# Moving the addition of D into the filter from VectorE to GpSimd, with a new order of all instructions

## Chip, cores and metric

The kernel runs on one core of one Trainium2 chip. The metric is the device time of one execution in microseconds (us). The core has TensorE (PE, matrix products), VectorE (DVE), ScalarE (ACT), GpSimd (POOL) and SyncE (SP), which here only issues transfers (DMA). The engines run side by side, each through its own list of instructions in order, and wait for each other by semaphores.

## What is computed

Two branches share one normalized input. Branch A is a short convolution of `k` with four taps, times `v`, and then a causal convolution along the whole sequence of 2048 with a filter `ssm_k` per channel, computed by FFT in the reference. A skip term `kv * ssm_D` is added to it. Branch B is a gated feed-forward layer with 1792 hidden columns.

```python
def _A_ref(q, k, v, shift_k, ssm_k, ssm_D):
    ...
    kv = k_shift * v
    ...
    y = irfft(rfft(pad(kv)) * rfft(pad(ssm_k)))[:S]      # shortened
    y = y + kv * ssm_D[None, None, :]
    return q * y

def _B_ref(x, w_gate, w_up, w_down):
    g = x @ w_gate; u = x @ w_up                          # shortened
    return (_gelu(g) * u) @ w_down

xn = _layernorm(A_q)
s = _A_ref(xn, A_k, A_v, A_shift_k, A_ssm_k, A_ssm_D)
g = _silu(_B_ref(xn, B_w_gate, B_w_up, B_w_down))
return A_q + s * g
```

Adding `kv * ssm_D` to a convolution is the same as adding `ssm_D` to the filter's first coefficient. The kernel does that: before the filter is transformed, D (512 values) is added to its row 0.

## The kernel before

The sequence is laid out as 128 partitions by 16 tiles. The feed-forward branch runs in four quarters `q` of four tiles each. A unit `(q, m)` is a pair of products for 128 hidden columns, `xnT` with `Wg` and with `Wu`, four matrix products each (both are recorded at the helper line L641); ScalarE applies gelu (L1194), VectorE multiplies (L1203 from PSUM, L1200 from a copy). `down(q)` multiplies with `Wd`, and L1235 and L1237 finish the gate.

The convolution is a Fourier transform in stages. The filter `Hn` is transposed on TensorE (L916) into `HTr`, evicted from PSUM by ScalarE (L632) or VectorE (L635). Stage 1 multiplies two-partition-halves of it with the matrix `F1` (L959 for the filter, in eight units; L950 for `kv`), with the array split in half ("half-array mode"); `ZH` and `ZK` are stored to memory in between (L614 issues, from ScalarE's queue for ZH and SP's for ZK) and loaded again as `BH` and `BK`. Stage 2 (L1028) uses 32 by 32 tiles of the array. VectorE multiplies the spectra (L1131, L1154), L1028 also goes back (`MI`), `ZI` is stored and loaded as `BI`, and L1278 ends the inverse.

`h_fold` (L930) is the addition of D. It works on one partition: 512 values of row 0 of `HTr`, every second element, and `Drow`. It needs the front evictions of all four blocks of the filter, and only the filter's unit 0 of stage 1 reads what it writes.

The short convolution has VectorE multiply and add over 2048 columns (L1005, L1009, L1011, L1013); its taps `SKB` are spread out by four GpSimd copies (L986) from `SKR`. The layer norm of quarter 0 goes tile by tile, the others by quarter: statistics (L849, L850, VectorE), `(var + eps)^-0.5` (L862, GpSimd), `NB_` (L866), the tile (L870 ScalarE or L871 VectorE), and a transpose into `xnT`: for quarter 0 on TensorE (L892), else by a DMA that SP issues (L884).

Nothing is ordered by loops when it runs. The functions add tasks to a list (`S.add`), each with the engines that it may use, a planned time, and the buffers that it reads and writes. `SEQ`, a string, lists all 809 tasks in the order in which they are emitted; the suffix `b` takes a task's second engine. So SEQ sets the order on every engine, SP's and ScalarE's queues of transfers included, and the engine of each eviction. `Sched.run` goes through it with planned times and from them picks the PSUM banks and buffer slots. `LAND` holds the times at which the planner takes each early load to have landed; the order of the loads stands in `ORDER`. Waits are derived from what is read and written (`Trk`).

Of the kernel before, what the change touches and what calls it, by code (L numbers as in the profile page):

```python
# [11 lines left out]
ALU = mybir.AluOpType  # L12
# [12 lines left out]
N_WARM = 13  # L25
ORDER = "x00 x01 w0 D0 h0 w1 h1 h2 h3 s0 k0 w2 x1 k1 k2 w3 d0 d1 v0 v1 k3 v2 v3 x2 x3"
SEQ = (
# [22 lines left out]
)  # L50
NF_BANKS = 4
ISSUE = 470.0
LAND = {"x0_0": 3800, "h0": 8050, "x0_1": 4900, "D": 6750, "wg0": 5850, "wu0": 6700, "h1": 12450, "wg1": 9600, "wu1": 11100, "h2": 13800, "h3": 15150, "sk": 17800, "kh1": 19200, "kh113": 19400, "kz": 10800, "k0": 20600, "wg2": 22500, "wu2": 24050, "x1": 25400, "k1": 26750, "k2": 28100, "wg3": 29650, "wu3": 31200, "wd0": 33450, "wd1": 35700, "v0": 37050, "v1": 38400, "k3": 39750, "v2": 41100, "v3": 42450}
W_XT, W_SW, W_BK, W_BH, W_ZI, W_BI, W_ZK, W_MI, W_G1 = 765000, 735000, 667000, 688000, 274000, 714000, 690000, 329000, 150000
NC_PAIRS = 4
SMALL = 1.15 * 262144
# [357 lines left out]
def build_kernel(nc, A_q, A_k, A_v, A_shift_k, A_ssm_k, A_ssm_D, B_w_gate, B_w_up, B_w_down, out):  # L414
    with ExitStack() as es0:
# [11 lines left out]
        def new(name, shape, dt):  # L427
            h = at(name, shape, dt, place["at"])
            place["at"] += size(shape, dt)
            return h  # L430
# [24 lines left out]
        Drow = new("Drow", [1, DM], BF16)  # L455
# [64 lines left out]
        def dsem(name):  # L520
            return DSem(nc.alloc_semaphore(name), name)
# [91 lines left out]
        def dma(eng, out_ap, in_ap, sem, r, w):  # L613
            trk.dma(eng, lambda e: e.dma_start(out=out_ap, in_=in_ap), sem, r=r, w=w)  # L614
# [3 lines left out]
        def load(name, out_ap, in_ap, w_res, w_buf, nbytes, ring="SP", r=(), rb=()):  # L618
            sem = dsem("d_" + name)
            last_load[0] = S.add([("loads", ISSUE)], lambda e: dma(ring, out_ap, in_ap, sem, r, w_res), r=rb, w=w_buf, nbytes=nbytes, land=float(LAND[name]))  # L620

        def op(engs, fn, r=(), w=(), rr=(), ww=(), lat=0.0, after=()):

            def emit(e):
                R = rr() if callable(rr) else rr
                W = ww() if callable(ww) else ww
                trk.op(e, lambda h: fn(e, h), r=R, w=W)
            return S.add(engs, emit, r=r, w=w, lat=lat, after=after)
# [297 lines left out]
        for k in range(KD):  # L926
            h_transpose(k)
        HT0 = HTr[0:1, 0, :].rearrange("p (d c) -> p c d", c=2)[:, 0, :]
        bFold = B("fold")
        h_fold = op([("DVE", 420.0)], lambda e, h: h.tensor_tensor(HT0, HT0, Drow[:], ALU.add),  # L930
                    r=[bHD, *[bHTr[k][0] for k in range(KD)]], w=[bFold], rr=[R_D, *R_HTr[0]], ww=R_HTr[0])
        t_ln = ln(0)
        S.add([("ACT", 1900.0)], m_turn, r=[bMF], w=[bMF2])
# [388 lines left out]
def bass_recurrent_scan__ssm_conv_h3__glu_gated_geglu__prompt_kernel(  # L1322
    nc: bass.Bass,
    A_q: bass.AP,
    A_k: bass.AP,
    A_v: bass.AP,
    A_shift_k: bass.AP,
    A_ssm_k: bass.AP,
    A_ssm_D: bass.AP,
    B_x: bass.AP,  # L1330
    B_w_gate: bass.AP,
    B_w_up: bass.AP,
    B_w_down: bass.AP,
    out: bass.AP,
):
    build_kernel(nc, A_q, A_k, A_v, A_shift_k, A_ssm_k, A_ssm_D, B_w_gate, B_w_up, B_w_down, out)
# [28 lines left out]
```

## Time and profile before

| what | value |
|---|---|
| median of 3 runs | 189.29 us (189.12 to 190.32) |
| profiled execution, its own time | 189.28 us |
| its span, first to last instruction | 187.5 us |
| granted TensorE clock | 0.999 |
| TensorE / VectorE / ScalarE / GpSimd busy | 97% / 88% / 75% / 7% |
| moved by DMA | 48.37 MB |

In the profile, PE rows are matrix products and PEld rows weight loads. A row of the timeline gives start and duration in us, engine, line of the kernel, operation, and what is written and read; `x4` means four such instructions merged. Matrix products overlap, so the durations of neighbouring rows do too, and starts are the better measure. `<-` in brackets names what ended an idle time. A row that ends with "DMA to landing" gives the times from the issue of a transfer until its data was there.

### The profile page before, as it was taken

What the parts mean: (1) busy time and instruction counts of PE and PEld (TensorE: products, weight loads), DVE (VectorE), ACT (ScalarE), POOL (GpSimd) and SP (SyncE); (2) the same over time, 40 slices, a digit from 0 to 9 for tenths busy, and PEclk for the clock granted to TensorE, in tenths of its full rate; (3) what the DMA queues carried; (4) which work ended last, traced back from release to release, by engine and by line L of the source; (5) the groups of instructions that cost most, each with busy time, mean ns of one, the idle gap of its engine ahead of it and who ended that gap; (6) DMA issues with size and microseconds to landing.
All of it is one profiled execution on the core that took longest, in us unless ns stands there. A gap on an engine that the chain in (4) does not pass through costs nothing.

```text
span 187.5 us, 3669 instructions
## 1 busy us (share of the span) xinstructions
PE 182.2 (97%) x1451; PEld 80.5 (43%) x1459; DVE 164.8 (88%) x249; ACT 140.0 (75%) x193; POOL 12.9 (7%) x26
## 2 busy tenths in 40 slices
PE   8899999999999999999999999999999999999993
PEld 3585443444334344334434433434333334445552
DVE  6897999999999999969459999998899994468995
ACT  3766697898698979888878779888887863144961
POOL 4502304100000000020200000000000000000000
PEclk9999999999999999999999999999999999999999
DMA  5999999999938695777999991869327056699226
GB/s 156 352 404 299 373 374 377 394 404 245 326 87 330 225 337 212 241 260 241 290 268 261 352 343 65 298 229 334 108 111 277 0 168 217 228 325 385 83 101 235
DMA packets 38502, 48.37 MB, mean 258 GB/s; under 512 B 9427, under 2 KB 28119, under 8 KB 38486
## 3 DMA queue, kind: packets, MB, share of 16 engines
q1 hardware_dynamic: 31958, 39.76, 64.1%
q10 hardware_dynamic: 6528, 8.39, 12.6%
q8 instruction: 11, 0.18, 0.5%
q14 instruction: 5, 0.04, 0.1%
HBM read 27.39 MB, written 14.68 MB: 224 GB/s over the span
## 4 chain that ended last, share of the span: by engine, by line
PE 91%; DVE 3%; DMA 2%; ACT 1%; issue 1%; POOL 0%
PE psall L641 71%; PE psall L1224 6%; PE psall L1028 6%; PE psall L950 2%; PE psall L959 2%; PE psall L916 2%; PE psall L1278 2%; DMA X<-in_A_q_dram 2%; ACT BO L632 1%; DVE stats L849 1%; DVE KAC L1005 1%; PE psall L892 0%; DVE XN L871 0%; DVE XN L965 0%; DVE HT L1203 0%
## 5 line engine op out<-in xcount | busy, mean ns | idle before, releaser
L641 PE MATMUL psall<-xnT,Wu 128*128 128x512 bf16 (+1 forms) x248 | 56.5, 359 | 0.0
L641 PE MATMUL psall<-xnT,Wg 128*128 128x512 bf16 (+1 forms) x248 | 55.8, 359 | 0.0
L1194 ACT ACTIVATE GE<-psall 128x512 bf16<-128x512 f32 x54 | 31.9, 606 | 13.6 <-PE psall L641 11.1
L641 PE MATMUL psall<-Wd,HT 128*128 128x512 bf16 (+1 forms) x174 | 38.3, 367 | 0.8 <-issue 0.6
L1203 DVE TENSOR_TENSOR HT<-psall,GE 128x512 bf16<-128x512 f32 x43 | 29.3, 682 | 7.8 <-PE psall L641 7.5
L641 PEld LDWEIGHTS psall<-xnT,Wu 128*128 128x128 bf16 x248 | 22.5, 98 | 26.1 <-issue 2.3
L641 PEld LDWEIGHTS psall<-xnT,Wg 128*128 128x128 bf16 x248 | 21.8, 98 | 26.0 <-issue 3.2
L632 ACT ACTIVATE BO<-psall 128x1024 bf16<-128x1024 f32 x20 | 19.9, 1022 | 9.4 <-PE psall L1278 4.8
L641 PEld LDWEIGHTS psall<-Wd,HT 128*128 128x128 bf16 x182 | 16.3, 98 | 21.2 <-issue 3.9
L1131 DVE TENSOR_TENSOR HSW<-KB,HSW 128x2048 bf16<-128x2048 bf16 x16 | 19.3, 1218 | 1.9 <-ACT KB L632 1.9
L632 ACT ACTIVATE HSW<-psall 128x1024 bf16<-128x1024 f32 x15 | 15.2, 1024 | 2.4 <-PE psall L1028 2.1
L632 ACT ACTIVATE KB<-psall 128x1024 bf16<-128x1024 f32 x15 | 14.6, 1026 | 0.8 <-PE psall L1028 0.8
L1011 DVE TENSOR_TENSOR KAC<-KAC,KTM 128x2048 bf16<-128x2048 bf16 x12 | 14.6, 1217 | 0.0
L1009 DVE TENSOR_TENSOR KTM<-KK,SKB 128x2048 bf16<-128x2048 bf16 x12 | 14.6, 1215 | 0.0
L632 ACT ACTIVATE AST<-psall 128x1024 bf16<-128x1024 f32 x12 | 12.1, 1032 | 0.9 <-PE psall L950 0.8
L1224 PE MATMUL psall<-Wd,HT 128*64 128x512 bf16 (+1 forms) x112 | 12.5, 366 | 0.0
L862 POOL TENSOR_TENSOR mv<-mv,NHALF 128x1 f32<-128x1 f32 (+1 forms) x7 | 7.3, 1049 | 68.6 <-DVE mv L850 48.0
L1235 ACT ACTIVATE G<-psall 128x512 bf16<-128x512 f32 x12 | 7.1, 597 | 6.3 <-PE psall L641 6.3
L849 DVE BATCH_NORM_STATS2 stats<-X 128x6 f32<-128x512 bf16 x16 | 10.5, 675 | 0.5 <-DMA X<-in_A_q_dram 0.5
L632 ACT ACTIVATE XN<-psall 128x1024 bf16<-128x1024 f32 x9 | 9.2, 1028 | 1.1 <-PE psall L959 1.0
L1237 DVE SCALAR_TENSOR_TENSOR G<-G,psall 128x512 bf16<-128x512 bf16 x12 | 7.9, 682 | 2.3 <-ACT G L1235 2.3
L1131 DVE TENSOR_TENSOR KB<-KB,HSW 128x2048 bf16<-128x2048 bf16 x8 | 9.7, 1219 | 0.1
(91 smaller groups left out, 178.3 us busy)
## 6 DMA issues: line engine op xcount, KB each, us to landing
BH<-ZH SPq DMA_DIRECT2D x8, 512.0 KB, 5.0
HSW<-HSW SPq DMA_DIRECT2D x16, 256.0 KB, 3.7
BK<-ZK SPq DMA_DIRECT2D x8, 512.0 KB, 5.9
ZI<-BO ACTq DMA_DIRECT2D x16, 256.0 KB, 2.8
BI<-ZI SPq DMA_DIRECT2D x8, 512.0 KB, 8.5
ZK<-AST SPq DMA_DIRECT2D x6, 512.0 KB, 2.9
ZH<-XN ACTq DMA_DIRECT2D x5, 512.0 KB, 4.3
Hn<-in_A_ssm_k_dram SPq DMA_DIRECT2D x4, 512.0 KB, 8.0
```

Source lines behind the costliest of these rows:

```text
L632: return h.activation(o, i, ACTF.Copy, scale=scale)
L641: return h.matmul(o, lhsT=l, rhs=r, start=st, stop=sp)
L849: t_stats[t] = op([("DVE", 670.0)], lambda e, h, t=t: h.bn_stats(stats[:, t, :], X[:, t, :]), r=[bX[q][t % 4]], w=[bst[t]], rr=[R_X[t]], w ...
L862: t_pw = op([("POOL", 2500.0 if q else 600.0)], lambda e, hd, ts=ts, n=n: hd.tensor_tensor(mv[:, ts, 3:4], mv[:, ts, 2:3], NHALF[:, 0:n, : ...
L1009: op([("DVE", dur)], lambda e, h, j=j, m=m: h.tensor_tensor(KTM[:, m.slot, :, :], kk(j), sk(j), ALU.mult), r=need + [bSKB[j], a], w=[m], r ...
L1011: op([("DVE", dur)], lambda e, h, m=m: h.tensor_tensor(KAC[:, a.slot, :, :], KAC[:, a.slot, :, :], KTM[:, m.slot, :, :], ALU.add), r=[m], ...
L1028: trk.op("PE", lambda h: h.matmul(ps(s, i)[b, :], lhsT=wt(col)[a, :], rhs=data(col)[a, :], start=n < 16, stop=n >= len(todo) - 16, tile_po ...
L1131: return hd.tensor_tensor(pair(KB, *(2 * DM * z for z in slots())) if to else x, k, x, ALU.mult)
L1194: op([("ACT", act(512))], lambda e, h: h.activation(GE[:, g.slot, :], bank(pg), ACTF.Gelu_apprx_tanh), r=[pg], w=[g], rr=lambda: R_bank(pg ...
L1203: op([("DVE", dve(512, 1))], lambda e, h: h.tensor_tensor(HT[:, q % 2, m, :], bank(pu), GE[:, g.slot, :], ALU.mult), r=[pu, g], w=[bHT[q][m]],
L1224: trk.op("PE", lambda h, m=m, i=i, c=c: h.matmul(pc()[c, :], lhsT=HT[:, q % 2, m, 128 * jt + 64 * i:128 * jt + 64 * i + 64], rhs=Wd[:, m, ...
L1237: op([("DVE", dve(512, 1))], lambda e, h, g=g, pc=pc: h.scalar_tensor_tensor(out=g, in0=g, scalar=1.0, in1=pc(), op0=ALU.add, op1=ALU.mult ...
```

## The change

Three things change in the program's text. `h_fold` may only run on GpSimd instead of only on VectorE (with a planned 1200 ns). `LAND` gets other planned landings for the first loads; `ORDER` and so the order of the loads stays. `SEQ` is another list of the same 809 tasks.

```diff
 SEQ = (
-    "0 16 17 18 19 20 21 22 ... 44 45 2 4 1 7 3 5 10 8 11 65 9 66 73b 74 12 67 68 76 77 75 6 69 "
...
+    "0 16 17 18 19 20 21 22 ... 44 45 2 7 10 4 8 1 9 3 11 6 65 66 67 68 5 73b 74 76 77 12 75 69 "
...
-LAND = {..., "h0": 8050, ..., "sk": 17800, "kh1": 19200, "kh113": 19400, ..., "k0": 20600, "wg2": 22500, "wu2": 24050, "x1": 25400, "k1": 26750, "k2": 28100, ...}
+LAND = {..., "h0": 8150, ..., "sk": 17450, "kh1": 18600, "kh113": 18850, ..., "k0": 20100, "wg2": 21600, "wu2": 23100, "x1": 24400, "k1": 25650, "k2": 27000, ...}
...
-        h_fold = op([("DVE", 420.0)], lambda e, h: h.tensor_tensor(HT0, HT0, Drow[:], ALU.add),
+        h_fold = op([("POOL", 1200.0)], lambda e, h: h.tensor_tensor(HT0, HT0, Drow[:], ALU.add),
```

Beside the fold, 25 tasks change engine between VectorE and ScalarE, nearly all of them evictions from PSUM and normalized tiles. On GpSimd the fold comes after the four SKB copies and before the first L862 of four columns; the two identity matrices, and the four copies among themselves, change places. On TensorE the first three tasks stay, and from the fourth on the order differs by up to 24 places. On SP, the loads of BH and the transfers of the spectra (HW, BK, ZK) change places in part: BH for spectrum block 5 now comes ahead of the first two BK instead of behind the transpose of quarter 3.

More of the change, by code (lines that the diff above doesn't have):

```diff
@@ L52 @@
 ISSUE = 470.0
-LAND = {"x0_0": 3800, "h0": 8050, "x0_1": 4900, "D": 6750, "wg0": 5850, "wu0": 6700, "h1": 12450, "wg1": 9600, "wu1": 11100, "h2": 13800, "h3": 15150, "sk": 17800, "kh1": 19200, "kh113": 19400, "kz": 10800, "k0": 20600, "wg2": 22500, "wu2": 24050, "x1": 25400, "k1": 26750, "k2": 28100, "wg3": 29650, "wu3": 31200, "wd0": 33450, "wd1": 35700, "v0": 37050, "v1": 38400, "k3": 39750, "v2": 41100, "v3": 42450}
+LAND = {"x0_0": 3850, "h0": 8150, "x0_1": 4950, "D": 6750, "wg0": 5800, "wu0": 6650, "h1": 12450, "wg1": 9650, "wu1": 11150, "h2": 13750, "h3": 15050, "sk": 17450, "kh1": 18600, "kh113": 18850, "kz": 10800, "k0": 20100, "wg2": 21600, "wu2": 23100, "x1": 24400, "k1": 25650, "k2": 27000, "wg3": 29650, "wu3": 31200, "wd0": 33450, "wd1": 35700, "v0": 37050, "v1": 38400, "k3": 39750, "v2": 41100, "v3": 42450}
 W_XT, W_SW, W_BK, W_BH, W_ZI, W_BI, W_ZK, W_MI, W_G1 = 765000, 735000, 667000, 688000, 274000, 714000, 690000, 329000, 150000
```

44 rows, old and new, of the table SEQ are left out of this document.

## The prediction

> **What bounds the kernel now.** I read the page's first two parts and its chain, then the busy time by windows, then what TensorE itself waited for.
>
> ```profile
> span 187.5 us, 3669 instructions
> PE 182.2 (97%) x1451; PEld 80.5 (43%) x1459; DVE 164.8 (88%) x249; ACT 140.0 (75%) x193; POOL 12.9 (7%) x26
> PEclk9999999999999999999999999999999999999999
> ...
> PE 91%; DVE 3%; DMA 2%; ACT 1%; issue 1%; POOL 0%
> ```
>
> TensorE (PE) is busy for 97% of the span at full granted clock, and the chain that ended last is TensorE for 91%. VectorE (DVE) is second with 88%, so it can make TensorE wait for a moment, but it isn't the bound. The windows show how little idle time there is to win (columns: stretch and its length, then each engine's busy time):
>
> ```profile
> 7.20:23.20 16.00, 15.96 (x146) 11.01 (x146) 13.86 (x27) 10.02 (x17) 4.01 (x6) 1.00 1.05 358
> ...
> 168.70:184.60 15.90, 15.90 (x159) 8.85 (x158) 14.93 (x27) 10.52 (x12) 0.00 (x0) 1.00 0.57 211
> sum 177.40, PE 176.20 PEld 78.56 DVE 158.54 ACT 135.74 POOL 9.10; mean PE 35.24 PEld 15.71 DVE 31.71 ACT 27.15 POOL 1.82
> ```
>
> From 7.2 us to its last product TensorE is idle for 177.40 - 176.20 = 1.2 us. Ahead of 7.2 us lies the first wait of the waits of TensorE:
>
> ```profile
> PE psall L892 <- DVE XN L871: 0.5, 1, 0.5
> PE psall L959 <- DVE HT L1203: 0.3, 1, 0.3
> ```
>
> The first, 0.5 us, is the second normalized tile; VectorE does the same work in the same order up to that tile in both versions, and GpSimd only makes its second identity earlier, in the 2.3 us that it waits ahead of the first L862 (its row is below), so it stays. The second is where VectorE is late. Any new order is therefore played for 1.2 us of idle time, plus what TensorE loses when it changes its array mode, which the windows count as busy:
>
> ```profile
> 28.20 1.03 PE L641 MATMUL psall<-xnT,Wg 128*128 128x512 bf16 x4
> 29.07 1.03 PE L641 MATMUL psall<-xnT,Wu 128*128 128x512 bf16 x4
> 30.03 0.61 PE L959 MATMUL psall<-HTr,F 64*128 64x512 bf16 x4
> 30.57 1.04 PE L641 MATMUL psall<-xnT,Wg 128*128 128x512 bf16 x4
> ```
>
> Start to start, four full products take 29.07 - 28.20 = 0.87 us. Ahead of the half-array products of L959 it is 0.96, and these four (two passes of one product's 0.87/4 = 0.217) take 0.54 instead of 0.43. One visit to the half-array mode costs 0.09 + 0.11 = 0.20 us beside its products.
>
> **The change, part by part.** The terms are set against the profiled execution's own 189.28 us (span 187.5 and 1.8 around it), which is within 0.01 of the median of the runs, 189.29.
>
> *The fold leaves VectorE.* It is one instruction, and its queue ahead of the TensorE wait is this:
>
> ```profile
> 17.53 1.06 DVE L930 TENSOR_TENSOR HTr<-HTr,Drow 1x512 bf16<-1x512 bf16 x1
> 18.50 0.67 DVE L1203 TENSOR_TENSOR HT<-psall,GE 128x512 bf16<-128x512 f32 x1
> ...
> 23.16 0.67 DVE L1203 TENSOR_TENSOR HT<-psall,GE 128x512 bf16<-128x512 f32 x1
> 23.18 0.39 PE L959 MATMUL psall<-HTr,F 64*128 64x512 bf16 x2
> 23.88 0.39 PE L959 MATMUL psall<-HTr,F 64*128 64x512 bf16 x2 [0.31 <-DVE HT L1203]
> ```
>
> VectorE has no pause from the fold to the gating L1203 at 23.16. Without 1.06 us of work ahead of it the second L959 pair would start 23.88 - 23.18 - 0.22 = 0.48 us earlier. The new order also moves kinds of work between ScalarE and VectorE here, so the gain lies between 0 and 0.48; I take 0.2.
>
> *The fold arrives on GpSimd.* There it stands behind the four SKB copies and ahead of the first four-column power of L862. GpSimd's rows:
>
> ```profile
> 17.35 2.90 POOL L986 COPY SKB<-SKR 128x512 bf16<-128x512 bf16 x4 [8.09 <-DMA SKR<-in_A_shift_k_dram]
> 30.62 3.06 POOL L862 TENSOR_TENSOR mv<-mv,NHALF 128x4 f32<-128x4 f32 x1 [10.38 <-DVE mv L860]
> L862 POOL TENSOR_TENSOR mv<-mv,NHALF 128x1 f32<-128x1 f32 x4 | 2.3, 564 | 3.5 <-ACT mv L859 2.3 <-DVE mv L860 1.2
> ```
>
> No row has this shape on GpSimd. The bounds are its nearest two-input instructions, 0.56 us below and 3.06 us above; since the copies of 512 columns take about 0.7 each, I take 1.5. The fold can start at 17.35 + 2.90 = 20.25 and ends between 20.8 and 23.3. Its first reader, the front half of filter unit 0, is the 62nd task of TensorE in the new order (the 66th before). In the old order the 62nd task is the first of this row:
>
> ```profile
> 38.99 0.81 PE L641 MATMUL psall<-Wd,HT 128*128 128x512 bf16 x3
> ```
>
> Cover: from 23.3 to 38.99, over 15 us of other products; without it the fold's whole 0.56 to 3.06 us would fall on TensorE. The next GpSimd instruction isn't due before 30.62, over 7 us later. So its cost there is 0. No DMA moves with it.
>
> How it meets VectorE is another matter. The fold took 1.06 us on VectorE beside the copies, where its neighbour of the same width over all partitions, two-input and SBUF to SBUF, took 0.42; and the power at 30.62 took 3.06 us beside two long VectorE products:
>
> ```profile
> L1245 DVE TENSOR_TENSOR G<-G,XN 128x512 bf16<-128x512 bf16 x3 | 1.3, 418 | 0.0
> 30.46 1.20 DVE L1005 TENSOR_TENSOR KAC<-KK,SKB 128x2048 bf16<-128x2048 bf16 x1
> 31.60 1.21 DVE L1011 TENSOR_TENSOR KAC<-KAC,KTM 128x2048 bf16<-128x2048 bf16 x1
> ```
>
> The power ends at 33.68, 0.9 us after the second of them. The Trainium skill, SBUF - State Buffer, section "Who interferes with whom", says that VectorE with two SBUF inputs and a GpSimd instruction that reads SBUF exclude each other for a whole instruction, whichever issued first. By that rule, with which both rows agree, the fold could hold up VectorE by as much as it frees.
>
> Whatever the reason, a fold of 1.5 us that holds up VectorE for its length would turn the 0.2 us above into a loss; that is a rival below.
>
> *The plan's landings.* LAND only feeds the planner; no load is issued in another order. Its numbers put nothing on the chip by themselves: 0.
>
> *The order.* I compared both SEQ lists engine by engine, and laid the old one beside the trace. The first and the last of the 15 old visits to the half-array mode:
>
> ```profile
> 15.73 0.39 PE L959 MATMUL psall<-HTr,F 64*128 64x512 bf16 x2
> 78.22 0.61 PE L950 MATMUL psall<-V,F 64*128 64x512 bf16 x4
> ```
>
> TensorE keeps its 252 tasks; the new list visits that mode 13 times, the other modes as often as before. Two visits at 0.20 are -0.4 us. Nothing hides this: it is TensorE's own time. That is the surest term.
>
> At the end the cover is the same: after the last inverse product 61 products stand ahead of the first L1278 both times, so the ZI stores and BI loads have their 13 us.
>
> ```profile
> 159.97 5.25 SPq L614 DMA_DIRECT2D BI<-ZI x8
> 168.72 0.62 PE L1278 MATMUL psall<-BI,G 128*64 128x512 bf16 x4
> ```
>
> The place where the new order can lose is the SP queue near 95 us. There the third transpose of XN waits for four normalized tiles, and the spectrum load BK for TensorE's L1028 stands right behind it:
>
> ```profile
> 93.01 0.82 ACT L870 ACTIVATE XN<-X,NB__69,mv 128x512 bf16<-128x512 bf16 x1
> 95.12 1.02 ACT L632 ACTIVATE KB<-psall 128x1024 bf16<-128x1024 f32 x1
> 94.53 3.79 SPq L884 DMA_TRANSPOSE xnT<-XN  x1
> 98.37 1.13 SPq L614 DMA_DIRECT2D BK<-ZK  x2
> 94.52 0.43 PE L1028 MATMUL psall<-BK,TF 32*32 32x512 bf16 x16
> 104.99 0.43 PE L1028 MATMUL psall<-BK,TF 32*32 32x512 bf16 x16
> DMA to landing us min/median/max: 5.9/5.9/5.9
> DMA to landing us min/median/max: 4.0/4.0/4.0
> ```
>
> The last two rows are the landing of the first BK at 98.37 and of an earlier BK at 86.62. Before, BK lands at 98.37 + 5.9 = 104.2 and TensorE takes it at 104.99. In the new order one normalized tile (XN9) stands on ScalarE behind the eviction of the L1028 of 94.52. That L1028 itself moves up by the five products that now follow it, 5 x 0.217 = 1.1 us, to 93.4. Its eviction by ScalarE (1.02 in the row of KB, begun some 0.4 after the product, once ScalarE's own instruction before it is done) ends near 94.9, XN9 (0.82) near 95.7; the transpose is issued 1.2 us later than before, BK at 99.6, and it lands between 99.6 + 4.0 = 103.6 and 99.6 + 5.9 = 105.5. TensorE comes there at 104.99 less what it has won by then, 104.4 with -0.6. The new wait is 0 to 1.1 us; the middle of the landings, 104.5, gives 0.1. One 512 KB load that stood between the two transposes (BH, issued at 92.21 before) now goes ahead of both, which speaks for the lower half; I take 0.2. Behind that wait stand all of TensorE's products; what is late next is nothing, since the BK loads after it have more room.
>
> *Sum.* 189.28 - 0.4 (two visits) - 0.2 (fold's queue) + 0.2 (BK) = **188.9 us**.
>
> **The rivals.**
>
> *Everything kept.* The wait at 23.88 vanishes whole and BK is in time: 189.28 - 0.4 - 0.48 = **188.4**. For it: both are shown in rows. Against it: the old order, made in the same way, has one such wait, and this one would have none.
>
> *BK decides (the other side).* If it lands at 105.5, TensorE goes on at 105.5 whatever it has won before, for it only waits longer: 189.28 + 105.5 - 104.99 = **189.8**. The deciding point is an issue of the transpose later than about 94.9: past that each microsecond is one of the end. For it: XN9 behind the eviction; against it: the smaller queue.
>
> *The move doesn't do what it says.* The fold on GpSimd blocks VectorE for its 1.5 us in the same stretch, and the L1203 of 23.16 comes up to 1.5 - 1.06 = 0.4 later: 189.28 - 0.4 + 0.4 = **189.3**. For it: the stretched rows. Against it: the copies leave gaps, and nothing says that the same L1203 gates TensorE in the new order.
>
> *PSUM hand-overs.* Many results change engines, and a bank that waits for one more eviction in an engine's queue costs 1.0 us (the row of KB). The old order shows one such wait in 252 tasks. Three of them would be 189.28 - 0.4 + 3 x 1.0 = **191.9**; the traces can't exclude it.
>
> **How the numbers follow.** Forecast as summed 0.47; everything kept 0.16; BK decides 0.15; fold blocks VectorE 0.10; hand-overs 0.10; better than 187.4, 0.02. A change of 1% is 1.9 us, and about what a measurement of this kernel can tell from no change; the runs shown lie from 189.12 to 190.32. Faster by that needs 187.4, that is all 1.2 us of idle time, the visits and part of the front wait together: 0.02. The first four cases are all within 1%: 0.88. Hand-overs: 0.10 for slower. The range goes from 188.1 (everything kept, and 0.3 of the other idle time) to 190.3 (BK decides and half an eviction more), with no more than 2 in 10 outside.
>
> **What would show it.** TensorE's groups L959 and L950 form 13 stretches; no TensorE wait on L1203 near 23 us, or a shorter one; one L930 on GpSimd ending before 24 us with no waiter; the third transpose issued near 95.7, BK's L1028 within 0.5 us of 104.5; TensorE idle 0.9 to 1.6 us after 7.2. The forecast is wrong if TensorE's idle time there exceeds 3 us, if a filter unit waits for L930, or if the number of stretches hasn't fallen.

## The result and the profile after

The changed kernel takes **191.59 us** (median of 6 runs, 190.86 to 194.89), the kernel before 189.38 beside it (6 runs, 189.06 to 190.32). The ratio is 1.0123, 95% interval 1.0096 to 1.015: slower by 1.2%, against a forecast of 188.9 and a range that ended at 190.3. (The ratios in this document are of undisturbed runs alone, so they can lie below the ratio of the medians.) The profiled execution took 191.84 us, span 190.1, 2.6 more than before.

The waits of TensorE, first view of after (columns: who waits, for what; us in total, times, longest):

```profile
PE psall L892 <- DVE XN L871: 1.2, 2, 0.7
PE psall L1028 <- ACT BO L632: 1.1, 1, 1.1
PE psall L641 <- PEq L1350: 0.8, 1, 0.8
PE psall L959 <- ACT X L632: 0.6, 1, 0.6
...
PE psall L959 <- ACT GE L1194: 0.2, 1, 0.2
PE psall L916 <- DMA Hn<-in_A_ssm_k_dram: 0.2, 1, 0.2
```

The wait for VectorE's L1203 that before had on L959 is gone, as predicted. Three waits for evictions stand in its place, into X, into BO and into GE. (The 0.7 us more on XN costs nothing: it lies ahead of the first normalized tile, where TensorE has run only products of a constant, and the first product of data starts at 6.38 us, at 6.32 before.) The busy time by windows says where they lie. First before (columns: stretch and its length, busy time of PE, PEld, DVE, ACT and POOL, granted clock, DMA share, GB/s):

```profile
7.20:40.00 32.80, 32.40 (x223) 18.22 (x225) 30.34 (x53) 24.67 (x38) 7.08 (x7) 1.00 1.06 372
40.00:56.00 16.00, 15.95 (x81) 6.20 (x80) 16.00 (x21) 13.56 (x21) 0.00 (x0) 1.00 0.86 248
56.00:124.00 68.00, 67.63 (x546) 27.11 (x547) 60.63 (x87) 57.56 (x79) 2.03 (x2) 1.00 0.81 264
124.00:136.00 12.00, 12.00 (x128) 4.75 (x127) 10.92 (x13) 9.84 (x14) 0.00 (x0) 1.00 0.67 223
```

The same stretches of after, with the sum up to the same distance from the end:

```profile
7.20:40.00 32.80, 32.11 (x222) 17.94 (x222) 29.13 (x50) 26.74 (x43) 7.06 (x8) 1.00 1.06 374
40.00:56.00 16.00, 15.26 (x74) 6.36 (x75) 15.45 (x20) 11.27 (x16) 0.00 (x0) 1.00 1.04 260
...
124.00:136.00 12.00, 10.90 (x122) 4.26 (x121) 10.59 (x12) 9.26 (x13) 0.00 (x0) 1.00 0.66 225
...
sum 180.00, PE 176.68 PEld 78.82 DVE 159.06 ACT 136.37 POOL 9.09; mean PE 35.34 PEld 15.76 DVE 31.81 ACT 27.27 POOL 1.82
```

TensorE's idle time from 7.2 us to its last product is 180.00 - 176.68 = 3.3 us; before it was 1.2. Of the 2.1 us more, 0.3 come by 40 us, 0.7 from 40 to 56, and 1.1 from 124 to 136. (TensorE's busy time, 176.68 instead of 176.20, makes up the rest of the 2.6.) The chain of work that ended last, from 40 to 51 us of after (start, us, what), shows what is behind the middle one:

```profile
40.83 0.92 ACT X L632
...
41.78 8.03 DMA ZH<-X
...
49.83 1.03 ACT X L632
...
50.91 0.39 PE psall L959
```

Halves of X and XN serve as the four buffers from which the filter's units are stored (H buffers). The store of unit 6 (ZH6) out of a half of X is issued at 41.78 and takes 8.03 us. Only then may ScalarE evict the next unit (ps1H4) into that half, and TensorE's second pair of unit 7 waits for the bank that this eviction frees. In the chain of before there is nothing but TensorE in this stretch: there the same store was issued at 43.35 and had landed after 4.2 us, at 47.6, when its buffer was asked for at 47.96.

A second profile of the same kernel has the same wait, longer, and the BO wait shorter:

```profile
PE psall L959 <- ACT X L632: 2.3, 1, 2.3
...
PE psall L1028 <- ACT BO L632: 0.5, 1, 0.5
```

### The profile page after: what moved, and what is told of

Same layout as the page of the kernel before. It is cut to its first block, busy times and chain, and to the rows that moved or that the text cites. A ratio compares the mean times of both kernels' runs of the same rounds, so it can differ in the third digit from the quotient of the medians.

```text
span 190.1 us, 3675 instructions
## 1 busy us (share of the span) xinstructions
PE 182.0 (96%) x1449; PEld 80.7 (42%) x1459; DVE 165.2 (87%) x247; ACT 140.6 (74%) x194; POOL 13.0 (7%) x27
## 4 chain that ended last, share of the span: by engine, by line
PE 75%; DMA 10%; ACT 6%; DVE 4%; SPq 3%; issue 1%; ACTq 0%
PE psall L641 57%; PE psall L1224 6%; DMA Hn<-in_A_ssm_k_dram 6%; PE psall L1028 6%; DMA ZH<-X 4%; SPq L614 3%; PE psall L950 2%; PE psall L1278 2%; ACT BO L632 2%; ACT XN L870 1%; DVE KTM L1009 1%; PE psall L959 1%; ACT X L632 1%; ACT GE L1194 1%; DVE stats L849 1%
## 5 line engine op out<-in xcount | busy, mean ns | idle before, releaser
L641 PE MATMUL psall<-xnT,Wu 128*128 128x512 bf16 (+1 forms) x248 | 55.8, 359 | 0.0
L641 PE MATMUL psall<-xnT,Wg 128*128 128x512 bf16 (+1 forms) x248 | 55.7, 359 | 0.0
L641 PE MATMUL psall<-Wd,HT 128*128 128x512 bf16 (+1 forms) x172 | 38.5, 366 | 0.8 <-issue 0.5
L1203 DVE TENSOR_TENSOR HT<-psall,GE 128x512 bf16<-128x512 f32 x43 | 29.3, 684 | 9.9 <-PE psall L641 9.4
L1194 ACT ACTIVATE GE<-psall 128x512 bf16<-128x512 f32 x54 | 31.3, 603 | 8.7 <-PE psall L641 5.2
L641 PEld LDWEIGHTS psall<-xnT,Wu 128*128 128x128 bf16 x248 | 22.1, 98 | 26.8 <-issue 3.5
L641 PEld LDWEIGHTS psall<-xnT,Wg 128*128 128x128 bf16 x248 | 22.0, 98 | 26.1 <-issue 2.3
L641 PEld LDWEIGHTS psall<-Wd,HT 128*128 128x128 bf16 x182 | 16.4, 98 | 20.8 <-issue 2.7
L632 ACT ACTIVATE BO<-psall 128x1024 bf16<-128x1024 f32 x21 | 20.9, 1024 | 5.1 <-PE psall L641 2.1
L632 ACT ACTIVATE KB<-psall 128x1024 bf16<-128x1024 f32 x14 | 13.9, 1028 | 3.7 <-PE psall L1028 3.6
L1235 ACT ACTIVATE G<-psall 128x512 bf16<-128x512 f32 x12 | 7.0, 596 | 12.1 <-PE psall L641 12.1
L632 ACT ACTIVATE HSW<-psall 128x1024 bf16<-128x1024 f32 x14 | 13.8, 1026 | 1.5 <-PE psall L1028 1.4
L862 POOL TENSOR_TENSOR mv<-mv,NHALF 128x1 f32<-128x1 f32 (+1 forms) x7 | 6.2, 885 | 66.2 <-DVE mv L860 63.1
L1154 DVE TENSOR_TENSOR HSW<-HSW 128x2048 bf16<-128x2048 bf16 x8 | 9.6, 1216 | 0.0
```

Source lines behind the costliest of these rows:

```text
L632: return h.activation(o, i, ACTF.Copy, scale=scale)
L641: return h.matmul(o, lhsT=l, rhs=r, start=st, stop=sp)
L1154: return hd.tensor_tensor(x, x, y, ALU.add)
L1194: op([("ACT", act(512))], lambda e, h: h.activation(GE[:, g.slot, :], bank(pg), ACTF.Gelu_apprx_tanh), r=[pg], w=[g], rr=lambda: R_bank(pg ...
L1203: op([("DVE", dve(512, 1))], lambda e, h: h.tensor_tensor(HT[:, q % 2, m, :], bank(pu), GE[:, g.slot, :], ALU.mult), r=[pu, g], w=[bHT[q][m]],
```

## The experiments

The theory I began with: new waits behind stores, in the order and not in the fold's engine. The first rival: the fold on GpSimd. The second: ScalarE's queue itself.

**After, taken again.** Nothing is edited.

> The changed kernel once more. Theory (stores): its loss is made of single waits of TensorE, 1.2 us near 132 us and 0.8 us near 50 us, both behind a ScalarE eviction that waits for the buffer of a slow store, 0.6 us near 31 us, and up to 1.0 us ahead of 18 us from loads that land late; the waits at 132 and 50 come again in this profile, at about their sizes, and the time is again 191 to 192. Rival (chance of one execution): the waits stand elsewhere or are gone, and the time of the profile isn't explained by them. Whether the filter blocks land at 9.4/13.7/15.0/16.8 us again, or at 8.1/12.4/13.7/15.0 as before the change, tells whether the early 1.0 us belongs to the change.

192.22 us (190.73 to 195.24, 6 runs), ratio 1.0109 (1.0081 to 1.0138). The loss is not one run's. Its two rows stand above: the waits come again at the same places, but not at the sizes expected, 2.3 us near 50 us and 0.5 near 132. The late landings at the front that the first profile had (0.2 us on L916) did not come back.

**The fold alone, both ways.** In after the fold goes back to VectorE; in before it goes to GpSimd:

```
-        h_fold = op([("POOL", 1200.0)], lambda e, h: h.tensor_tensor(HT0, HT0, Drow[:], ALU.add),
+        h_fold = op([("DVE", 420.0)], lambda e, h: h.tensor_tensor(HT0, HT0, Drow[:], ALU.add),
```

> The changed kernel with its new order, and the fold back on VectorE. Theory (the order's waits): the fold's engine is not the cause, 191.0 to 192.0, and the waits near 50 and 132 us stay. Rival (the fold on GpSimd holds VectorE up): most of the loss is gone, 189.4 to 190.0, and the wait near 31 us is gone.

> The kernel before with its old order, and the fold alone on GpSimd behind the four copies. Theory: no loss; VectorE has 1 us less to do ahead of 23 us, so the wait there (0.48 us) shrinks: 188.8 to 189.4. Rival (the fold on GpSimd costs by itself): 190.5 or more.

After's order with the fold on VectorE: 192.15 us (191.53 to 194.08, 6 runs), ratio 1.0165 (1.0125 to 1.0204). Before's order with the fold on GpSimd: 190.1 us (189.56 to 190.78, 12 runs), ratio 1.0035 (1.0021 to 1.0049). So the slowdown stays when the fold's move is undone, and the move alone costs 0.4 to 0.9 us on the old order, between what the theory and the rival had. The wait for L1203 is still there in that profile, 0.37 us at 24.2. Why the move gains nothing is in two rows of the timeline of before with the fold on GpSimd:

```profile
20.12 1.15 POOL L930 TENSOR_TENSOR HTr<-HTr,Drow 1x512 bf16<-1x512 bf16 x1
...
20.47 1.95 DVE L965 TENSOR_TENSOR XN<-XN 128x1024 bf16<-128x1024 bf16 x2
```

And in the line of the product L1005 in after (duration in ns, least, median and most):

```profile
L1005 DVE TENSOR_TENSOR KAC<-KK,SKB x4: 1211/1214/2179, 21.4 to 61.5; 128x2048 bf16<-128x2048 bf16 x4
```

The pair of L965 took 1.27 us in the kernel before and takes 1.95 beside the fold. In after the product L1005 that begins at 21.4, under the fold on GpSimd, takes 2.18 us instead of 1.21. VectorE gets 1.06 us of work less and is held for 0.7 to 0.97. (Why the move costs something beyond that, these rows don't show.) The Trainium skill, SBUF - State Buffer, section "Who interferes with whom", has the rule for it, an exclusive lock between VectorE with two SBUF inputs and GpSimd; both traces agree with it.

**More buffers.** Two more output buffers of the inverse (BO), then one more for the filter's spectra, then both:

```
-        BO = at("BO", [128, 4, 2, DM], BF16, ast_at)
+        BO4 = at("BO", [128, 4, 2, DM], BF16, ast_at)
+        BO2 = at("BOX", [128, 2, 2, DM], BF16, kk_at - 2048)
...
+        HX = at("HX", [128, 2, 2, DM], BF16, g_at + 8192)
```

> The changed kernel with six buffers instead of four for the evicted inverse products (BO), so that the eviction near 131 us need not wait for the store issued at 125.3 us. Theory (stores): the wait of 1.2 us near 132 us is gone and the time falls by 0.8 to 1.3, to about 190.4. Rival (ScalarE's queue is late there, the eviction's place in the order is what costs): the wait stays and the time is the changed kernel's within 0.3.

> After with a fifth buffer for the half-transformed H blocks (HX, 8 KB a partition, in space that is free then), so that the eviction of ps1H7_0 near 50 us need not wait for the store of ZH5 out of X. Theory 'one store': in all four profiles of this order that store took 8.0 to 10.1 us and TensorE lost 1.0 to 3.1 us behind it before ps1H7_1; so here that loss is 0, the TensorE wait on ScalarE into X is gone, the median is 189.8 to 190.5, and no run is above 191.5 or shows a granted clock under 0.995 (the runs of 193 to 195 us with clocks of 0.99 would be those where this wait was longest). The wait at psf3_0 near 132 us stays, 0.8 to 1.6 us, since TensorE comes there earlier. Rival 'ScalarE late': the wait moves to another instruction by 52 us and the median stays at 191.3 or above.

> After with both the fifth H buffer and six instead of four buffers for the inverse's output. Theory 'stores': both waits behind stores (before ps1H7_1 and before psf3_0) are gone at once; TensorE's lost time falls from 4.6 to 4.9 us to 2.2 to 2.6, and the median is 188.8 to 189.5, level with the kernel before or 0.4 below it. Rival 'given back': one wait taken away makes another longer (as six buffers alone did: 194.3 us), and the median is 190.5 or above.

Six BO: 194.3 us (191.68 to 195.82, 6 runs), ratio 1.017 (1.0124 to 1.0215). Five H buffers: 191.72 (189.93 to 196.12, 8 runs), ratio 1.0102 (1.0064 to 1.0141). Both: 191.93 (189.94 to 193.73, 10 runs), ratio 1.0106 (1.0066 to 1.0146). All three missed what I expected. Each wait went where its buffer was added, but the time did not come back. (Two expectations call the store ZH5 and the held eviction that of ps1H7_0; the store is ZH6's, and in after's order the eviction is ps1H4_0's, which goes into that buffer, and ps1H7_1 is what TensorE then can't start.) TensorE's waits with five H buffers show one way, in an execution of 196.12 us (a kernel with more lines has other line numbers, here L642 for L641):

```profile
PE psall L642 <- DMA xnT<-XN: 4.4, 1, 4.4
```

TensorE no longer waits for an eviction into X; it waits 4.4 us for the transposed tile of the second quarter, xnT1. Its transpose took 15.6 us in this profile (9.0 in before); in after it took 9.6 and in the second profile 12.1, and the wait behind the store had hidden it. So the buffer is not all there is to it: two transfers that are in flight together are both late. With both kinds of buffers the profiled execution took 190.1 us, and none of these waits is in it; what its executions of 192 to 193 us waited for was not profiled.

**The sequence of the transposes.** SP issues three more DMA transposes near there. I put them back into the sequence of before (G1, MI1, MI0 are steps 178, 180, 179 of the order):

```
-  137 179 138 ... 99 178 506 ... 534 180 477
+  137 178 138 ... 99 180 506 ... 534 179 477
```

> After with the three DMA transposes of the filter's spectra issued in the sequence of before (G1, MI1, MI0 instead of MI0, G1, MI1); all else as in after, four H buffers. Theory 'transposes': the store of ZH5 is slow because MI0's transpose runs beside that of xnT1 (both move small packets: 186 GB/s at a full DMA share from 45 to 50 us, 347 before); here the store takes 3.7 to 5.5 us, xnT1's transpose 8 to 9.7 instead of 9.6 to 12.4, the wait before ps1H7_1 is under 0.2 us, and the median is 189.8 to 190.5. Rival 'early': the store is slow because it is issued at 41 us, while the last loads of V are still landing, and not at 43 to 45; here it still takes 7 us or more, and the median stays at 191.0 to 192.3.

192.04 us (191.37 to 195.79, 5 runs), ratio 1.0126 (1.0101 to 1.0151); the wait behind the store was 3.0 us in its profile, of an execution of 195.79 us. The theory on the transposes' sequence fell. Its rival, the time at which the store is issued, was left.

**One repair more.** With both kinds of buffers and the transposes in the old sequence, VectorE's product HT0_9 (step 422) goes ahead of the long ktm0_1 (149):

```
-  463 149 421 416 406 408 63 466 415 422 464
+  463 421 416 406 408 63 415 422 149 466 464
```

> As the kernel with both buffers, with the transposes in the sequence of before, and one VectorE step moved: the product of gate and up tile HT0_9 ahead of the K filter's ktm0_1 (1.2 us) near 28.7 us, so that the GE buffer it frees no longer holds ScalarE's eviction ge0_5 to 30.55 us and TensorE 0.6 us before psu0_7. Theory 'order': all three are repaired; TensorE loses 1.5 to 2.0 us beside its products and the median is 188.2 to 189.0, below the kernel before. Rival: the moved step delays the K filter and the loss comes out elsewhere, 189.4 or above.

190.62 us (189.52 to 191.45, 12 runs), ratio 1.0044 (1.0017 to 1.0071). Better by 1.0 than after, but not below before: TensorE still waited 1.4 us for xnT1.

**When the store is issued.** The DMA rows from 44 to 50 us of before (GB/s in slices of 0.15 us; packets, MB, mean GB/s; then by queue: q1 is SP's with the transposes, q10 ScalarE's with the stores: packets, MB, share of 16 engines):

```profile
GB/s 22 31 22 266 294 283 295 287 290 292 290 357 401 437 396 423 437 423 382 382 356 423 437 423 410 369 382 410 442 202 13 0 177 259 423 410 341 355 423 396
DMA packets 2503, 1.90 MB, mean 317 GB/s; under 512 B 1787, under 2 KB 1787, under 8 KB 2503
...
q10 hardware_dynamic: 748, 1.47, 64.5%
q1 hardware_dynamic: 1755, 0.43, 32.6%
...
xnT<-XN SPq DMA_TRANSPOSE x1, 9.0
```

The same view of after:

```profile
GB/s 15 17 147 292 294 302 288 304 186 73 68 87 61 68 77 60 123 314 302 108 106 159 130 77 89 164 104 96 423 423 423 437 396 382 358 404 389 399 369 266
DMA packets 2165, 1.32 MB, mean 220 GB/s; under 512 B 1731, under 2 KB 1731, under 8 KB 2165
...
q1 hardware_dynamic: 1711, 0.43, 58.7%
q10 hardware_dynamic: 454, 0.89, 58.0%
...
xnT<-XN SPq DMA_TRANSPOSE x1, 9.6
```

As many transpose packets, 0.43 MB both times, take 58.7% of the engines' time instead of 32.6%. A share of 16 engines over 6 us, divided by the packets: 0.326 x 96 / 1755 = 0.018 us for each packet of q1 before, 0.587 x 96 / 1711 = 0.033 after; for q10 0.083 before and 0.123 after. The engines are full and move less. The slices show where: before, the transposes run first at 266 to 295 GB/s and the store behind them at 350 or more; in after the rate falls from about 300 to between 60 and 190 from 45.2 to 48.2 us (but for two slices), while both queues have packets on the engines. The last load of V is not what slows them: it is issued at 32.8 us and has landed 11.7 us later, at 44.5. What differs in the queues is when the store is issued. The transpose of xnT1 and the ZH6 store in before:

```profile
38.75 5.69 SPq L884 DMA_TRANSPOSE xnT<-XN  x1
43.35 0.37 ACTq L614 DMA_DIRECT2D ZH<-X  x1
```

And in after:

```profile
40.36 4.33 SPq L884 DMA_TRANSPOSE xnT<-XN  x1
41.78 0.37 ACTq L614 DMA_DIRECT2D ZH<-X  x1
```

The store comes 4.6 us behind the transpose in before and 1.4 us behind it in after. The crossed test moves that one store in each order. In before, step 135 goes ahead; in after, 135 and 105 (ZH1) go behind the eviction 127:

```
-  436 425 125 95 ... 451 85 135 96 443
+  436 425 135 125 95 ... 451 85 96 443
```

```
-  442 126 135 451 ... 104 105 152 98 153 443 127 476
+  442 126 451 ... 104 152 98 153 443 127 135 105 476
```

> Before with one step moved: ScalarE issues the store of ZH6 straight after the eviction ge0_10, near 41 us, instead of near 43.4; nothing else differs. Theory 'mixing': a store whose packets come to the DMA engines among those of xnT1's transpose slows both (in the order of before the transpose's packets of 256 B ran alone and took 0.018 us each, and the store's of 2 KB alone 0.084; in the order of after they were mixed and took 0.04 to 0.12 and 0.12 to 0.27). So here xnT1's transpose takes 11 to 13 us instead of 9.0, the store 7.5 to 10 instead of 4.2, the eviction of ps1H7_0 waits for the store 1 to 3 us, and the median is 190.5 to 192.5, with single runs at 193 or above. Rival 'order': the place of this one store costs nothing by itself, median 189.2 to 189.8.

> After with two steps moved: ScalarE issues the stores of ZH6 and ZH1 behind the eviction of ps1H5_1, near 45.2 us, instead of at 41.0 and 43.7; still four H buffers. Theory 'mixing': xnT1's transpose runs ahead of both stores and lands by 48.5 us (8 to 9.5 us), the stores take 4 to 5 us each; the eviction of ps1H7_0 still waits for ZH6 (to 49.5 us, 1.0 to 1.6 us for TensorE), but evenly: median 190.3 to 191.0, no run above 192 and none with a granted clock under 0.995. Rival 'order': transpose and stores stay at 8 us or more and the median at 191.3 to 192.3.

Before with the store early: **192.03 us** (190.65 to 195.29, 6 runs), ratio 1.0107 (1.0064 to 1.0149). After with the stores late: **190.8 us** (190.26 to 192.65, 12 runs), ratio 1.0075 (1.0047 to 1.0104). Both medians are where "mixing" put them; two of the twelve runs with late stores went above the 192 that I had set, and the wait for ZH6 that I still expected there (1.0 to 1.6 us) is gone: the store took 4.4 us, the transpose 9.9 and not 8 to 9.5. The interval of the late stores overlaps those of after (1.0096 to 1.015, 1.0081 to 1.0138). The DMA rows of the same 6 us of before with the early store:

```profile
DMA packets 1843, 0.87 MB, mean 145 GB/s; under 512 B 1621, under 2 KB 1621, under 8 KB 1842
...
q1 hardware_dynamic: 1615, 0.41, 75.4%
q10 hardware_dynamic: 227, 0.45, 39.3%
...
xnT<-XN SPq DMA_TRANSPOSE x1, 11.5
```

And of after with the late stores:

```profile
DMA packets 2888, 1.92 MB, mean 320 GB/s; under 512 B 2224, under 2 KB 2224, under 8 KB 2888
...
q10 hardware_dynamic: 689, 1.35, 57.8%
q1 hardware_dynamic: 2199, 0.57, 41.8%
...
xnT<-XN SPq DMA_TRANSPOSE x1, 9.9
```

One step moved in the old order takes it from 317 GB/s to 145, and a transpose packet from 0.018 us to 0.754 x 96 / 1615 = 0.045; two steps moved in the new order bring back 320 GB/s and 0.018. TensorE's waits in before with the early store (no such line in before):

```profile
PE psall L959 <- ACT X L632: 1.5, 2, 0.9
...
PE psall L916 <- DMA Hn<-in_A_ssm_k_dram: 1.1, 1, 1.1
```

The store took 10.3 us there. After 7.2 us TensorE is idle for 2.7 us more than in before: 1.6 of them lie from 40 to 56 us, behind the store, and 1.0 is the second row, a filter block that landed late, near 9 us, which a step moved near 41 us doesn't explain. So in this profile the store's place is worth 1.6 us.

The Trainium skill, DMA: Bandwidth & Descriptors, section "Queues, rings and completion order", says that each DMA engine takes turns between the queues that have work for it, packet by packet. That two queues share the engines here agrees with it; that the turns cost so much beside a transpose is what these rows add.

**The late stores with the other repairs.**

> The late stores with the fifth H buffer. Theory 'mixing': no wait before ps1H7_1 and none for xnT1 near 55 us (4.4 us with the fifth buffer and early stores); median 189.5 to 190.2, no run above 191. Rival: xnT1 still lands after 51 us and TensorE waits for it, 191 or above.

> The late stores with five H buffers, six output buffers of the inverse and the earlier product HT0_9. Theory 'mixing': all the waits of the new order are gone; TensorE loses 1.5 to 2.2 us and the median is 188.3 to 189.1, below the kernel before (189.6). Rival: something else of this order holds it, 189.6 or above.

With five H buffers: 191.92 us (190.5 to 192.21, 7 runs), ratio 1.0103 (1.0067 to 1.0139), a miss: the mixing was gone (343 GB/s from 44 to 50 us), and the profile shows 1.6 us on BO at 132 us instead of 0.2. With everything: 189.89 us (189.05 to 191.09, 12 runs), ratio 1.0023 (1.0001 to 1.0045), above the 188.3 to 189.1 that I expected. Its windows, in an execution of 189.05 us:

```profile
40.00:56.00 16.00, 15.95 (x80) 6.47 (x80) 16.00 (x20) 11.77 (x17) 0.00 (x0) 1.00 0.93 273
56.00:124.00 68.00, 67.15 (x541) 26.81 (x542) 61.45 (x89) 55.83 (x75) 2.03 (x2) 1.00 0.87 261
124.00:136.00 12.00, 12.00 (x142) 4.69 (x141) 11.42 (x14) 10.21 (x14) 0.00 (x0) 1.00 0.53 183
...
sum 177.20, PE 175.83 PEld 78.65 DVE 157.95 ACT 135.97 POOL 8.59; mean PE 35.17 PEld 15.73 DVE 31.59 ACT 27.19 POOL 1.72
```

The stretches from 40 to 56 and from 124 to 136 are full again. But from 56 to 124 us TensorE is now idle for 0.85 us instead of 0.37 in before: the waits have one of 0.4 on VectorE's product of gate and up there, which after doesn't have, where TensorE came later. Its busy sum is 0.37 below before's.

**The fold, once more, with the repairs in place.** The fold on VectorE ahead of the K filter's first product (step 64 ahead of 146):

```
-  116 101 146 ... 419 407 111 414 467 64 465
+  116 101 64 146 ... 419 407 111 414 467 465
```

> After's order with the late stores, six output buffers of the inverse, the earlier product HT0_9 (four H buffers), and the fold back on VectorE, put ahead of the K filter's first product kac0. Theory 'fold neutral for VectorE': on GpSimd it held that product at 2.18 us instead of 1.21 in both profiles of after, as much as the fold takes on VectorE (1.06); so here VectorE's row shows 1.06 for the fold and 1.2 for kac0, the same end, and the time is that of the other repairs: 189.0 to 189.8. Rival 'fold helps on GpSimd': 0.3 or more above the kernel with the fold on GpSimd (189.89 with all the repairs), 190.2 or above.

> As the kernel with all repairs (late stores, five H buffers, six output buffers, earlier HT0_9; 189.89), but the fold on VectorE ahead of kac0. Theory 'fold neutral': 189.2 to 190.1, kac0 1.2 us. Theory 'fold costs on GpSimd' (0.6 us, as the fold alone did in the order of before): 189.0 to 189.4. Rival 'fold helps on GpSimd': 190.2 or above. With four or five H buffers the time is the same within 0.4 us if the ZH6 store lands before the eviction that needs its buffer (48.0 us against 48.05 with four buffers and late stores).

190.46 us (189.41 to 195.98, 12 runs), ratio 1.0042 (1.0017 to 1.0067), with four H buffers; 190.47 us (189.76 to 192.16, 12 runs), ratio 1.005 (1.0022 to 1.0077), with five. VectorE's rows are as "neutral" had them: the product behind the fold takes 1.20 us in both, the fold 0.72 and 1.18. But both times lie where the rival "fold helps on GpSimd" put them, 190.2 or above, and against 1.0023 (1.0001 to 1.0045) with the fold on GpSimd the intervals overlap. So this stays open: on before's order the move cost 0.35%, here it may help by 0.2 to 0.3%, and in neither order is it worth a whole microsecond. No version here beats the kernel before.

## Why the prediction was wrong

**The step that failed is the claim that the place where the new order can lose is SP's queue near 95 us.** The sum has no term for ScalarE's queue of stores, and the ZH stores appear in no row of the prediction. The sum put that wait at nothing; in the two profiles of after the stretch from 40 to 56 us, where it stands, lost 0.7 and 2.4 us. The store's place moved alone in before costs 2.0 us by the ratio (1.2 to 2.8) and 1.6 in its profile; moved back in after it wins 0.6 to 0.9 us by the ratios (1.0075 against 1.0123 and 1.0109), which the intervals don't fully separate. It is a large part and not the whole: a wait for a BO buffer near 132 us took 1.1 and 0.5 us in the same two profiles, and six BO buffers take that wait away.

**The right rival was priced, but for another reason.** PSUM hand-overs at 191.9 with 0.10: banks did wait for evictions. That the time is within 0.3 us is luck: the sum had three waits of 1.0 us, and the two profiles have 1.1, 0.6 and 0.2, and 2.3, 0.5 and 0.2. I had taken one eviction of 1.0 us as the price of each. What the runs showed is that evictions are held by the store that must leave their buffer, so the price is a store's time in contention (8.0 us for ZH6, and in the second profile 2.3 us of TensorE's wait behind it), not an eviction's.

**BK: no loss.** SP's queue in after:

```profile
97.14 1.76 SPq L884 DMA_TRANSPOSE xnT<-XN  x1
98.95 1.96 SPq L614 DMA_DIRECT2D BK<-ZK  x2
```

TensorE's rows of the same timeline:

```profile
104.55 1.89 PE L641 MATMUL psall<-xnT,Wg 128*128 128x512 bf16 x8
106.37 0.43 PE L1028 MATMUL psall<-BK,TF 32*32 32x512 bf16 x16
```

The transpose went out at 97.14, not at 95.7, but TensorE came later too, and its L1028 begins without a pause at 106.37. The term of 0.2 was 0; the rival on BK didn't occur. In the kernel with all the repairs, where TensorE isn't late, the transpose goes out at 95.78 and the L1028 begins at 104.70 without a wait, about as the prediction had it.

**The visits: held in number.** There are 13 in after, the first at 18.02 us and the last at 79.59. Their 0.4 us is not shown: where the waits are gone the busy sum is 175.83 against 176.20, but other kernels with 13 visits have sums of up to 177.8 at full clock, and the traces don't have every product on record (1432 to 1442 of them from 7.2 us on). So "the surest term" stays an estimate from the price of one visit.

**The fold: its cost right, its gain not.** It took 1.67 us on GpSimd (predicted 1.5) with no waiter, and the wait on L1203 is gone. But the VectorE time that it frees is taken back by the hold, so the term of -0.2 belongs to the order and not to the fold: the wait is still there with the fold alone moved (0.37 us at 24.2), and near 23 us it is gone with the new order and the fold on VectorE. The rival "fold blocks VectorE" had the mechanism, 0.97 us of it, and as a cause of this slowdown it is out: the fold back on VectorE left 192.15.

**What stays open.** How the remaining waits trade against each other: buffers alone moved time about and won none on the median. Nor do the runs show why a store issued 4 us behind a transpose lets it pass, though both are then in flight, while one issued 1 to 1.4 us behind it doesn't. With all the repairs the new order is level with the old one to 0.2%, not 0.4 us faster.

## What to carry over

When an order is made anew, follow every queue that issues transfers, ScalarE's too, and ask of each store which eviction needs its buffer next and what else moves on the DMA engines in that time; a busy share of 1.0 says nothing without the GB/s beside it. A resource that shows up as the releaser may only be the first of two that are late: if a buffer is added and the wait moves to another transfer, look at what both share. Price a new order by the gaps it may open, not by those it closes: the old one had 1.2 us of idle time to win and far more to lose.

## What the runs showed of the hardware

A plain store among the packets of a DMA transpose cuts what the engines move, at a full share: over the 6 us to 145 and 220 GB/s from 317 to 320, and in most slices of the mixed stretch to between 60 and 190, where the transposes alone move some 290 and the store alone some 400.

After a long wait TensorE's granted clock halves. With five H buffers and the 4.4 us wait (columns as above, the clock ahead of the last two):

```profile
50.00:54.00 4.00, 0.72 (x3) 0.16 (x2) 2.23 (x3) 0.97 (x2) 0.00 (x0) 0.92 1.11 271
54.00:58.00 4.00, 2.80 (x7) 1.02 (x8) 2.96 (x3) 1.76 (x4) 0.00 (x0) 0.50 0.75 243
58.00:62.00 4.00, 4.00 (x14) 1.42 (x12) 1.83 (x2) 1.90 (x4) 0.00 (x0) 0.72 0.52 163
```

From 54 to 58 us the clock is 0.50, and it is 0.72 over the next 4. With the transposes in the old sequence a wait of 3.0 us had 0.57 behind it for 4 us; with six BO buffers it was 2.7 us and the clock stayed at 1.00. The Trainium skill, TensorE: Matmul & The Clock Gate, section "What's actually happening", puts the drop to half at about 3.4 us without work. The waits of 4.4 and 2.7 us agree with that; the one of 3.0 is shorter and had the drop behind it all the same. So a wait of some 3 us or more can cost more than itself. It may be how single executions of the new order come to 193 to 196 us: all of those have granted clocks of 0.98 to 0.991, as has the one execution of before above 193 (193.56 us, 0.991).
